# Sink attention and a routed attention mixture on one core: part of the loads and stores issued by ScalarE, other units by way of DRAM, and a new written-out order

## The chip, the cores and the metric

The kernel runs on one core of a Trainium2 chip. The core has a matrix engine (TensorE, in the profile PE, its weight loads PEld), a vector engine (VectorE, DVE), a scalar engine (ScalarE, ACT), a general engine (GpSimd, POOL) and an engine that here only issues transfers (SyncE, SP). Sixteen DMA engines move the data. An engine executes its instructions strictly in the order in which the program has them; across engines they wait for each other by semaphores. A transfer is started by an instruction that stands in the order of the engine that issues it.

The metric is the device time of one execution in microseconds (us), the median of some runs.

## The reference

Everything is float32, with inputs of 4 batches, 8 heads, 768 positions, head size 64. The first stage is a windowed attention in which each position sees the last 128 positions and the first 4 ("sinks"). Its output, heads side by side, is the input x (4 x 768 x 512) of the second stage: four "experts", each a causal attention with a head size of 64, weighted by a gate that keeps two experts for each position.

```python
keep = is_sink | in_window                      # 4 sinks, window 128
a = softmax(where(keep, q @ k.T / 8, -1e9))
x = (a @ v)                                     # heads side by side: 4 x 768 x 512
logits = x @ w_gate                             # two of four experts kept per position
for e in range(4):
    q, k, v = x @ wq[e], x @ wk[e], x @ wv[e]
    s = where(causal, -1e9, q @ k.T / 8)
    ye = softmax(s) @ v @ wo[e]
    out += weight_of(e) * ye                    # 0 where e is not among the two
```

## The kernel before

**Units.** The work is cut into units. A unit of the first stage, written (b, hp, 0), is one batch and one pair of heads (16 of them); a unit of the second stage, (b, ep, 1), is one batch and one pair of experts (8). In this document (b, ep) alone is a unit of the second stage. Sequences are cut into six blocks of 128 positions ("rows"). The two heads or experts of a pair use the two halves of the matrix engine.

**First stage** (`first`, `band_rows`, `edge_rows`, `both_rows`). q, k and v of a pair are loaded into natural-order tiles `qn`, `kn`, `vn` (three, two and three buffers). For batch 0 PE turns q and k (L1425, against the identity), for later batches the load brings 32 x 32 pieces and DVE turns them (L1323). Scores of the blocks come from L1348 and L1366, DVE takes the minimum and adds the mask (L1642, L1704), ACT makes the exponentials (L1647, L1708), POOL or ACT normalise, PE turns the probabilities (L1425), DVE or ACT move them to SBUF as `pt`, and PE multiplies them with v (L1392) and the sinks (L1396).

**Second stage** (`second`, `values`, `wide_rows`). x is kept as a high and a low part, and every product with weights is made of three (high with high, high with low, low with high): L1799 for queries and keys, L1826 for values and gate, L1873 for the output. Scores are L1353, DVE's mask and minimum L1570, exponentials L1578.

**Rows by way of DRAM.** A row block's probabilities must be turned before they meet v. For most blocks PE does it (`transposed`: L1425, then an evacuation to `pt`). For blocks 3, 4 and 5 of the units in `AWAY` (`by_way_of_dram`) the normalised block goes to `u` (three buffers), DVE turns it in 32 x 32 pieces (L1515, two instructions), one transfer writes it to DRAM as `there` (L1518), four read it back rearranged (L1522), and PE multiplies it with v (L1392, written `b<-u,v` in the trace). Five units of three blocks do this: (0,0), (0,1), (1,0), (1,1), (2,0).

**What sets the order.** Nothing is ordered by hand. Each piece of work is a `Step` with a priority, a cost in ns on each engine that could do it, the steps and buffers that it needs, and for a transfer the time `moves` that the DMA engines would take. `Plan.emit` plays a list scheduling: the engine that can start a step earliest takes one, PE by priority with a penalty for waiting and for changing the shape in which it is used. The result is only an order for each engine (and, for steps with two engines, the choice of one); the chip then runs these orders as fast as it can. Priorities get a correction from the table `NUDGE`, and `ONLY` pins steps to one engine; both are tables of numbers found by search. `ISSUE` multiplies the cost of SP's issues. Where the plan finds PE idle in the first 130 us of its own time, it puts in dummy matmuls on a tile of zeros (`fill`, L1037 the wide form, L1040 the narrow one); their results are never used.

**Transfers.** All are issued by SP, in one order: loads of q, k, v (L1763, and L1767 for 32 x 32 pieces, four instructions each), weights (L1151), the trips to DRAM and back (L1518, L1522), stores of the output (L1877). An issue that waits holds everything behind it on SP.

Of the kernel before, what the change touches and what calls it, by code (L numbers as in the profile page):

```python
# [1981 lines left out]
```

## Time and profile before

| | us |
|---|---|
| median of 3 runs (lowest, highest) | 380.84 (379.81, 382.02) |
| the profiled execution | 381.89 |
| its span, first to last instruction | 379.1 |
| PE busy | 360.7 (95%) |
| DVE busy | 292.6 (77%) |
| ACT busy | 271.0 (71%) |
| POOL busy | 196.3 (52%) |
| mean granted clock of PE | 0.989 |
| DMA, share of the sixteen engines | 52.5% on the kernel's queue |

The page divides the span into 40 slices of 9.5 us and gives for each the busy tenths of an engine, the clock granted to PE in tenths and the share of the DMA engines. A group's row gives its line, engine, tile names, shapes and count, then busy time and the mean ns of one, then the idle time of the engine just before and what ended it. A row of the waits reads: who waited for whom, us in total, times, the longest. A matmul in float32 counts as two in the trace. Matmuls overlap, so the mean of one is longer than the pace at which they follow each other; the pace is read from the pieces of the chain of waits.

### The profile page before, as it was taken

To read this page: it belongs to the slowest core of one execution; us is meant where nothing else is said; L and a number is where in the kernel's file an instruction comes from. 1 tells how busy PE (TensorE), PEld (TensorE's weight loads), DVE (VectorE), ACT (ScalarE), POOL (GpSimd) and SP (SyncE) were. 2 spreads that over 40 slices of the span, in tenths; PEclk is the share of its full clock that TensorE was granted. 3 is DMA by queue.
4 is the path that set the end of the run, shared out by engine and by line. 5 is a ranking of instruction groups with operands and counts; after the bars stand their busy time and mean duration, and the time that the engine had idled before them with its cause. 6 is when DMAs were issued, how large, how long until landed. Compare 5 with 4: busy or idle time off the path is not lost.

```text
span 379.1 us, 12937 instructions
## 1 busy us (share of the span) xinstructions
PE 360.7 (95%) x4642; PEld 310.3 (82%) x4642; DVE 292.6 (77%) x1272; ACT 271.0 (71%) x943; POOL 196.3 (52%) x474
## 2 busy tenths in 40 slices
PE   8988989999979998999998998999999999999996
PEld 7767878887768897978887887988888989988884
DVE  4898769779978978879987996649888936484951
ACT  2998959449967987448986975437999835068872
POOL 4398977949338733654655863142498510123410
PEclk9996999999999999999999999999999999999999
DMA  7998899904895686548965695026910000030012
GB/s 159 189 194 146 165 177 172 155 2 109 284 186 93 175 262 110 86 122 292 206 157 95 155 261 141 3 108 227 254 43 3 4 0 29 2 117 24 3 58 111
DMA packets 134832, 48.10 MB, mean 127 GB/s; under 512 B 121776, under 2 KB 129456, under 8 KB 134768
## 3 DMA queue, kind: packets, MB, share of 16 engines
q1 hardware_dynamic: 134768, 47.28, 52.5%
q8 instruction: 36, 0.59, 0.7%
q14 instruction: 28, 0.23, 0.2%
HBM read 30.88 MB, written 16.12 MB: 124 GB/s over the span
## 4 chain that ended last, share of the span: by engine, by line
PE 63%; DMA 10%; DVE 9%; ACT 6%; SPq 5%; POOL 4%; issue 2%; DVEq 0%; ACTq 0%
PE b L1392 15%; PE b L1873 9%; PE b L1799 9%; PE b L1353 7%; PE b L1826 7%; PE b L1425 7%; DMA u<-there 4%; DMA qn<-in_q_dram 3%; SPq L1767 3%; PE b L1348 3%; PE b L1366 3%; DMA there<-u 3%; SPq L1522 2%; ACT p L1708 2%; DVE u L1515 2%
## 5 line engine op out<-in xcount | busy, mean ns | idle before, releaser
L1578 ACT ACTIVATE p<-p,st 128x640 f32<-128x640 f32 (+5 forms) x96 | 63.6, 665 | 14.2 <-DVE st L1570 11.4
L1708 ACT ACTIVATE p<-p,st 128x132 f32<-128x132 f32 x128 | 50.8, 400 | 8.3 <-DVE st L1704 6.2
L1570 DVE CUSTOM_DVE_ANT_0 p<-b,cmask 128x384 f32<-128x384 f32 (+3 forms) x96 | 45.4, 501 | 2.4 <-PE b L1353 2.1
L1353 PE MATMUL b<-ks,qs 64*128 64x384 f32 (+3 forms) x384 | 44.3, 342 | 1.1 <-DVE st L1570 0.6
L1222 ACT ACTIVATE pt<-b 128x256 f32<-128x256 f32 (+3 forms) x99 | 38.8, 421 | 5.7 <-PE b L1425 5.3
L1425 PE MATMUL b<-ident,p 64*128 64x64 f32 x820 | 39.4, 227 | 0.2 <-DVE y L1210 0.2
L1392 PE MATMUL b<-pt,vn 128*64 128x128 f32 x448 | 39.0, 280 | 0.6 <-ACT pt L1222 0.5
L1224 DVE COPY pt<-b 128x256 f32<-128x256 f32 (+3 forms) x75 | 32.1, 450 | 8.3 <-PE b L1425 7.4
L1425 PEld LDWEIGHTS b<-ident,p 64*128 64x128 f32 x820 | 32.6, 138 | 6.8 <-issue 2.5
L1826 PE MATMUL b<-wvh,x 128*128 128x260 f32 x192 | 37.6, 286 | 0.2 <-DVE x L1210 0.2
L1408 POOL TENSOR_TENSOR st<-st 128x2 f32<-128x2 f32 (+1 forms) x52 | 10.2, 197 | 51.7 <-ACT p L1578 27.9
L1353 PEld LDWEIGHTS b<-ks,qs 64*128 64x128 f32 x384 | 30.9, 186 | 5.4 <-issue 1.6
L1726 POOL TENSOR_TENSOR p<-p,st 128x512 f32<-128x512 f32 x32 | 33.1, 1040 | 0.1
L1873 PE MATMUL b<-woh,y 128*128 128x512 f32 x96 | 32.8, 400 | 0.0
L1799 PE MATMUL b<-x,wkh 128*128 128x256 f32 (+1 forms) x128 | 32.7, 343 | 0.0
L1799 PE MATMUL b<-x,wqh 128*128 128x256 f32 (+1 forms) x128 | 32.6, 342 | 0.0
L1826 PEld LDWEIGHTS b<-wvh,x 128*128 128x128 f32 x192 | 30.6, 188 | 1.6 <-issue 0.6
L1704 DVE CUSTOM_DVE_ANT_0 p<-b,pair_mask 128x132 f32<-128x132 f32 x128 | 31.7, 283 | 0.0
L1647 ACT ACTIVATE p<-p,st 128x256 f32<-128x256 f32 (+1 forms) x64 | 28.6, 450 | 1.8 <-DVE st L1642 1.4
L1392 PEld LDWEIGHTS b<-pt,vn 128*64 128x64 f32 x448 | 25.4, 136 | 3.1 <-ACT pt L1222 0.8
L1366 PE MATMUL b<-kx,qn 64*64 64x196 f32 (+2 forms) x768 | 27.2, 286 | 0.0
L1826 PE MATMUL b<-wvl,x 128*128 128x260 f32 x96 | 27.1, 282 | 0.0
(133 smaller groups left out, 993.1 us busy)
## 6 DMA issues: line engine op xcount, KB each, us to landing
vn<-in_v_dram SPq DMA_DIRECT2D x32, 192.0 KB, 3.8
out_dram<-o SPq DMA_DIRECT2D x24, 256.0 KB, 2.0
qn<-in_q_dram SPq DMA_DIRECT2D x52, 96.0 KB, 3.2
kn<-in_k_dram SPq DMA_DIRECT2D x52, 96.0 KB, 2.5
there<-u SPq DMA_DIRECT2D x5, 768.0 KB, 4.1
u<-there SPq DMA_DIRECT2D x20, 192.0 KB, 5.1
there<-u SPq DMA_DIRECT2D x5, 640.0 KB, 2.9
u<-there SPq DMA_DIRECT2D x20, 160.0 KB, 3.8
```

Source lines behind the costliest of these rows:

```text
L1222: nc.scalar.activation(dst(), src(), AF.Copy)
L1353: nc.tensor.matmul(o, self.qs.t[hs, a, qs], keys(hs, b), start=n == 0, stop=n == 2)
L1366: nc.tensor.matmul(o, self.q_of()[hs, q0 + 64 * h:q0 + 64 * h + 64], ks, start=True, stop=True)
L1392: nc.tensor.matmul(o[e * 64:e * 64 + 64], lhs, rhs, start=e not in self.begun, stop=last and self.done == len(self.steps))
L1425: nc.tensor.transpose(t[g].t[:, n, :], x[gs], ident[gs, gs])
L1570: nc.vector.tensor_tensor_reduce(out=one(e)[:, cs], in0=s2[e].t[:, :(c1 - c0) * 128], in1=mask(c0, c1), scale=times, scalar=st.t[:, 3, es] ...
L1578: nc.scalar.activation(x, x, AF.Exp, bias=st.t[:, 0, es], scale=-1.0, accum_out=st.t[:, 1, es])
L1708: nc.scalar.activation(p.t[:, n, :], p.t[:, n, :], AF.Exp, bias=st.t[:, 0, n:n + 1], scale=-1.0, accum_out=st.t[:, 1, n:n + 1])
L1726: nc.gpsimd.tensor_mul(p.t[:, :, :128], p.t[:, :, :128], f()[:, :, None].to_broadcast([128, 4, 128]))
L1799: nc.tensor.matmul(t.t, w[a][:, c, es], X[b, c].t[:, x, cs], start=c == 0 and m == 0, stop=c == NCH - 1 and m == 2)
L1826: nc.tensor.matmul(t.t[:, :VW], X[b, c].t[:, a, qs], W["wv"][w][:, c, :], start=c == 0 and n == 0, stop=c == NCH - 1 and n == 2)
L1873: nc.tensor.matmul(t.t, Y[b, c].t[:, a, qs], W["wo"][w][:, c, :], start=c == 0 and n == 0, stop=c == EP - 1 and n == 2)
```

## The change

1. A new helper `transfer` makes a step that either SP or ACT may take, and issues the transfer on the engine that the plan (or `ONLY`) gave it. Loads of q, k, v and of the weights and stores of the output use it; the trips to DRAM and back stay on SP.
2. In the plan an issue on SP costs 1.4 times its figure (before 1.2), every transfer's DMA time is multiplied by 1.25, the end of every transfer comes 400 ns later, and transfers by ACT occupy the plan's DMA time too. Some figures of issues change (four loads of 32 x 32 pieces 2580 for 2124, two loads 1100 for 1062, reading back 2000 for 1900).
3. `AWAY` names (1,0), (1,1), (2,0), (2,1), (3,0): units (0,0) and (0,1) now have their blocks turned by PE, (2,1) and (3,0) go by way of DRAM.
4. `NUDGE` and `ONLY` are new throughout, and so are three weights of the order (`HURRY`, `STAY`, `BULK`). So the order of all engines is made anew.

The products that PE computes are the same in kind and number. In the order of the changed kernel 49 transfer instructions stand on ACT (15 of the 24 stores, 34 of loads); narrow dummy matmuls are 82 instead of 52, wide ones besides the opening ten 4 instead of 1. Of the two tables the diff shows two lines.

```diff
-ISSUE = 1.2
+ISSUE, MOVE_TIME, LANDING = 1.4, 1.25, 400
...
 ONLY = {
-    "000 fn_DVEACT 0": DVE, "000 fn_DVEACT 2": ACT, "000 fn_DVEACT 5": ACT, "000 fn_DVEACT 6": ACT, "000 fn_DVEACT 7": DVE,
+    " load_SPACT 0": SP, " load_SPACT 4": SP, " load_SPACT 5": SP, "000 load_SPACT 0": ACT, "000 load_SPACT 1": SP,
...
-HURRY = 79.02
-STAY = 46.95
-BULK = 0.96
+HURRY = 86.86
+STAY = 50.53
+BULK = -58.78
...
-        self.prio, self.cost, self.fn, self.new, self.moves, self.mode = prio, cost, fn, new, moves, mode
+        self.prio, self.cost, self.fn, self.new, self.moves, self.mode = prio, cost, fn, new, moves * MOVE_TIME, mode
...
-            if e == SP:
+            if s.moves:
                 moved = max(moved, t + 1000) + s.moves
-                free[SP] = max(s.end, moved - 2500)
-                s.end = max(moved + 1000, s.end + 1800)
+                if e == SP:
+                    free[SP] = max(s.end, moved - 2500)
+                s.end = max(moved + 1000, s.end + 1800) + LANDING
...
+    def transfer(prio, many, each, fn, *rest, queues=(SP, ACT), **more):
+
+        def go():
+            fn((nc.scalar if s.eng == ACT else nc.sync).dma_start)
+        go.__qualname__ = fn.__qualname__
+        s = plan.step(prio, {q: many * each for q in queues}, go, *rest, **more)
+        return s
...
-            ld = plan.step(prio, {SP: 530 * many}, load, new=[st], fifo=tag, moves=2400 * whole / 1024)
+            ld = transfer(prio, many, 530, load, new=[st], fifo=tag, moves=2400 * whole / 1024)
...
-        got = plan.step(prio - WIDE_N - 10, {SP: 1900}, back, [s], (), [there, u], moves=2 * MOVE * n)
+        got = plan.step(prio - WIDE_N - 10, {SP: 2000}, back, [s], (), [there, u], moves=2 * MOVE * n)
...
-                loaded[-1].append((a, z, [plan.step(
-                    load_prio + (0.1 if n else 0.2 if which == 2 else 0), {SP: 1062 if which == 2 or by_pe else 2124}, load, (), [] if n else [t],
+                loaded[-1].append((a, z, [transfer(
+                    load_prio + (0.1 if n else 0.2 if which == 2 else 0), *((2, 550) if which == 2 or by_pe else (4, 645)), load, (), [] if n else [t],
...
-        plan.step(prio, {SP: 410}, lambda: nc.sync.dma_start(out[b, qs, :], o.t), [moved], (), [o], moves=650)
+        transfer(prio, 1, 410, lambda start: start(out[b, qs, :], o.t), [moved], (), [o], moves=650)
...
-    AWAY, MOVE = {u: (3, 4, 5) for u in ((0, 0), (0, 1), (1, 0), (1, 1), (2, 0))}, 250
+    AWAY, MOVE = {u: (3, 4, 5) for u in ((1, 0), (1, 1), (2, 0), (2, 1), (3, 0))}, 250
```

More of the change, by code (lines that the diff above doesn't have):

```diff
@@ new lines @@
+    "000 load_SPACT 2": SP, "000 load_SPACT 3": ACT, "000 load_SPACT 4": SP, "000 fn_DVEACT 1": ACT, "000 fn_DVEACT 3": ACT,
+    "000 fn_DVEACT 4": DVE, "000 fn_DVEACT 5": ACT, "000 fn_DVEACT 6": DVE, "000 fn_DVEACT 7": DVE,
+    "000 total_DVEPOOL 0": POOL, "000 norm_POOLACT 0": POOL, "000 norm_POOLACT 1": POOL, "000 fn_DVEACT 8": DVE,
+    "000 total_DVEPOOL 1": DVE, "000 fn_DVEACT 10": ACT, "000 fn_DVEACT 11": DVE, "000 fn_DVEACT 13": DVE,
+    "000 total_DVEPOOL 2": POOL, "000 fn_DVEACT 15": DVE, "000 fn_DVEACT 16": DVE, "000 fn_DVEACT 17": ACT,
@@ new lines @@
+    "030 fn_DVEACT 4": ACT, "030 fn_DVEACT 5": ACT, "030 fn_DVEACT 7": DVE, "030 norm_POOLACT 0": ACT,
+    "030 norm_POOLACT 1": ACT, "030 fn_DVEACT 8": ACT, "030 fn_DVEACT 10": ACT, "030 fn_DVEACT 12": DVE,
+    "030 fn_DVEACT 13": DVE, "030 total_DVEPOOL 2": DVE, "030 fn_DVEACT 14": DVE, "030 fn_DVEACT 15": DVE,
+    "030 fn_DVEACT 16": DVE, "030 fn_DVEACT 17": ACT, "110 load_SPACT 0": SP, "110 load_SPACT 1": SP,
+    "110 load_SPACT 2": SP, "110 total_DVEPOOL 0": DVE, "110 norm_POOLACT 0": POOL, "110 norm_POOLACT 1": ACT,
@@ new lines @@
+    "110 fn_DVEACT 0": DVE, "110 fn_DVEACT 1": ACT, "110 total_DVEPOOL 1": DVE, "110 fn_DVEACT 4": DVE,
+    "110 total_DVEPOOL 2": DVE, "110 fn_DVEACT 8": DVE, "110 fn_DVEACT 9": ACT, "100 load_SPACT 0": SP,
+    "100 load_SPACT 1": SP, "100 load_SPACT 2": ACT, "100 total_DVEPOOL 0": POOL, "100 norm_POOLACT 0": ACT,
+    "100 norm_POOLACT 1": POOL, "100 fn_DVEACT 1": ACT, "100 total_DVEPOOL 1": DVE, "100 fn_DVEACT 2": ACT,
+    "100 fn_DVEACT 3": ACT, "100 fn_DVEACT 6": ACT, "100 fn_DVEACT 8": ACT, "100 fn_DVEACT 9": ACT, "001 fn_DVEACT 1": ACT,
@@ new lines @@
+    "001 fn_DVEACT 2": ACT, "001 fn_DVEACT 3": ACT, "001 fn_DVEACT 4": ACT, "001 fn_DVEACT 5": DVE,
+    "001 norm_POOLACT 0": ACT, "001 norm_POOLACT 1": POOL, "001 fn_DVEACT 6": ACT, "001 norm_POOLACT 3": ACT,
+    "001 fn_DVEACT 9": DVE, "001 total_DVEPOOL 2": DVE, "001 norm_POOLACT 4": POOL, "001 norm_POOLACT 5": POOL,
+    "001 fn_DVEACT 11": ACT, "001 total_DVEPOOL 3": POOL, "001 norm_POOLACT 6": POOL, "001 norm_POOLACT 7": POOL,
+    "001 fn_DVEACT 12": DVE, "001 total_DVEPOOL 4": POOL, "001 norm_POOLACT 8": ACT, "001 norm_POOLACT 9": POOL,
@@ new lines @@
+    "001 fn_DVEACT 14": ACT, "001 fn_DVEACT 15": ACT, "001 total_DVEPOOL 5": DVE, "001 fn_DVEACT 18": DVE,
+    "001 fn_DVEACT 19": ACT, "001 fn_DVEACT 20": DVE, "001 fn_DVEACT 21": ACT, "120 load_SPACT 0": SP,
+    "120 load_SPACT 1": SP, "120 load_SPACT 2": ACT, "120 norm_POOLACT 0": POOL, "120 fn_DVEACT 0": DVE,
+    "120 total_DVEPOOL 1": DVE, "120 total_DVEPOOL 2": DVE, "120 fn_DVEACT 6": DVE, "120 fn_DVEACT 7": DVE,
+    "120 fn_DVEACT 8": ACT, "120 fn_DVEACT 9": ACT, "130 load_SPACT 0": SP, "130 load_SPACT 1": ACT,
@@ new lines @@
+    "130 load_SPACT 2": ACT, "130 total_DVEPOOL 0": POOL, "130 norm_POOLACT 0": ACT, "130 fn_DVEACT 0": DVE,
+    "130 fn_DVEACT 2": ACT, "130 fn_DVEACT 3": ACT, "130 fn_DVEACT 4": ACT, "130 fn_DVEACT 6": ACT, "130 fn_DVEACT 7": ACT,
+    "130 fn_DVEACT 9": DVE, "011 norm_POOLACT 1": ACT, "011 fn_DVEACT 0": DVE, "011 fn_DVEACT 1": ACT,
+    "011 fn_DVEACT 2": ACT, "011 total_DVEPOOL 2": POOL, "011 fn_DVEACT 4": ACT, "011 total_DVEPOOL 3": POOL,
+    "011 norm_POOLACT 7": POOL, "011 fn_DVEACT 6": ACT, "011 norm_POOLACT 9": ACT, "011 fn_DVEACT 11": DVE,
@@ new lines @@
+    "011 norm_POOLACT 10": POOL, "011 norm_POOLACT 11": ACT, "011 fn_DVEACT 12": ACT, "011 fn_DVEACT 13": DVE,
+    "011 fn_DVEACT 14": ACT, "011 fn_DVEACT 15": ACT, "011 fn_DVEACT 16": ACT, "011 store_SPACT 1": SP,
+    "011 fn_DVEACT 18": DVE, "011 fn_DVEACT 19": ACT, "011 store_SPACT 3": ACT, "011 fn_DVEACT 20": ACT,
+    "011 fn_DVEACT 21": ACT, "011 store_SPACT 5": ACT, "210 load_SPACT 1": SP, "210 load_SPACT 2": SP,
+    "210 total_DVEPOOL 0": DVE, "210 norm_POOLACT 0": POOL, "210 norm_POOLACT 1": POOL, "210 fn_DVEACT 0": DVE,
@@ new lines @@
+    "101 norm_POOLACT 5": POOL, "101 fn_DVEACT 6": DVE, "101 norm_POOLACT 6": ACT, "101 norm_POOLACT 7": POOL,
+    "101 total_DVEPOOL 4": POOL, "101 norm_POOLACT 9": POOL, "101 norm_POOLACT 10": ACT, "101 norm_POOLACT 11": ACT,
+    "101 fn_DVEACT 11": ACT, "220 load_SPACT 1": SP, "220 total_DVEPOOL 0": POOL, "220 norm_POOLACT 1": POOL,
+    "220 fn_DVEACT 0": ACT, "220 total_DVEPOOL 1": DVE, "220 fn_DVEACT 2": DVE, "220 fn_DVEACT 4": DVE,
+    "220 fn_DVEACT 5": ACT, "220 total_DVEPOOL 2": POOL, "220 fn_DVEACT 6": ACT, "220 fn_DVEACT 7": ACT,
@@ new lines @@
+    "230 load_SPACT 0": SP, "230 load_SPACT 1": ACT, "230 load_SPACT 2": SP, "230 fn_DVEACT 1": ACT,
+    "230 total_DVEPOOL 1": DVE, "230 fn_DVEACT 4": ACT, "230 fn_DVEACT 5": DVE, "230 fn_DVEACT 6": ACT,
+    "111 total_DVEPOOL 0": POOL, "111 norm_POOLACT 2": POOL, "111 norm_POOLACT 3": POOL, "111 total_DVEPOOL 2": DVE,
+    "111 norm_POOLACT 4": POOL, "111 fn_DVEACT 0": DVE, "111 fn_DVEACT 1": ACT, "111 total_DVEPOOL 3": POOL,
+    "111 norm_POOLACT 7": POOL, "111 norm_POOLACT 9": ACT, "111 fn_DVEACT 2": DVE, "111 fn_DVEACT 3": ACT,
@@ new lines @@
+    "111 total_DVEPOOL 5": POOL, "111 norm_POOLACT 10": ACT, "111 norm_POOLACT 11": POOL, "111 fn_DVEACT 5": ACT,
+    "111 fn_DVEACT 6": ACT, "111 store_SPACT 0": SP, "111 fn_DVEACT 7": DVE, "111 store_SPACT 1": ACT,
+    "111 fn_DVEACT 8": ACT, "111 fn_DVEACT 9": ACT, "111 store_SPACT 3": ACT, "111 fn_DVEACT 10": ACT,
+    "111 store_SPACT 4": ACT, "300 load_SPACT 0": SP, "300 load_SPACT 1": SP, "300 load_SPACT 2": ACT,
+    "300 norm_POOLACT 1": ACT, "300 fn_DVEACT 2": DVE, "300 fn_DVEACT 3": ACT, "300 fn_DVEACT 5": DVE,
@@ new lines @@
+    "201 fn_DVEACT 9": ACT, "201 total_DVEPOOL 5": DVE, "201 norm_POOLACT 11": POOL, "201 fn_DVEACT 10": DVE,
+    "201 fn_DVEACT 11": DVE, "310 load_SPACT 0": SP, "310 norm_POOLACT 0": ACT, "310 norm_POOLACT 1": POOL,
+    "310 fn_DVEACT 0": ACT, "310 fn_DVEACT 1": ACT, "310 fn_DVEACT 3": DVE, "310 fn_DVEACT 5": ACT,
+    "310 total_DVEPOOL 2": DVE, "310 fn_DVEACT 6": ACT, "310 fn_DVEACT 7": ACT, "310 fn_DVEACT 8": ACT,
+    "310 fn_DVEACT 9": ACT, "320 load_SPACT 0": SP, "320 load_SPACT 1": ACT, "320 load_SPACT 2": SP,
@@ new lines @@
+    "320 total_DVEPOOL 0": POOL, "320 fn_DVEACT 0": DVE, "320 fn_DVEACT 1": DVE, "320 total_DVEPOOL 1": DVE,
+    "320 fn_DVEACT 4": DVE, "320 fn_DVEACT 5": ACT, "320 fn_DVEACT 6": ACT, "320 fn_DVEACT 8": DVE, "320 fn_DVEACT 9": ACT,
+    "330 load_SPACT 0": SP, "330 load_SPACT 1": SP, "330 norm_POOLACT 0": POOL, "330 fn_DVEACT 0": ACT,
+    "330 total_DVEPOOL 1": POOL, "330 fn_DVEACT 3": ACT, "330 fn_DVEACT 5": ACT, "330 total_DVEPOOL 2": DVE,
+    "330 fn_DVEACT 6": ACT, "330 fn_DVEACT 8": ACT, "211 total_DVEPOOL 0": DVE, "211 norm_POOLACT 0": ACT,
@@ new lines @@
+    "211 fn_DVEACT 10": ACT, "211 store_SPACT 4": SP, "211 fn_DVEACT 11": ACT, "301 fn_DVEACT 1": DVE,
+    "301 fn_DVEACT 2": DVE, "301 fn_DVEACT 4": ACT, "301 fn_DVEACT 5": ACT, "301 norm_POOLACT 1": ACT,
+    "301 norm_POOLACT 2": POOL, "301 norm_POOLACT 3": POOL, "301 norm_POOLACT 4": ACT, "301 norm_POOLACT 5": POOL,
+    "301 total_DVEPOOL 3": POOL, "301 norm_POOLACT 7": POOL, "301 total_DVEPOOL 4": POOL, "301 norm_POOLACT 8": POOL,
+    "301 norm_POOLACT 9": POOL, "301 fn_DVEACT 8": DVE, "301 total_DVEPOOL 5": POOL, "301 norm_POOLACT 10": ACT,
@@ L1758, in first, with load @@
             for n, (a, z) in enumerate([(0, 3), (3, NB)] if whole and which < 2 else [(0, NB)]):
-                def load(t=t, src=src, which=which, a=a, z=z):
+                def load(start, t=t, src=src, which=which, a=a, z=z):
                     for e in range(2):
@@ L1762, in load @@
                         if which == 2 or by_pe:
[L1763 removed]
+                            start(t.t[:, a:z, e, :], x.rearrange("(t p) d -> p t d", p=128)[:, a:z, :])
                             continue
```

142 lines of the change are left out of this document (45 added, 97 removed), and 1333 rows, old and new, of the table NUDGE.

## The prediction

> **What bounds the kernel now.** I read the page's shares first, then the clock and DMA lines of its slices, then PE's waits, then the stretches in which PE is not full.
>
> ```profile
> PE 360.7 (95%) x4642; PEld 310.3 (82%) x4642; DVE 292.6 (77%) x1272; ACT 271.0 (71%) x943; POOL 196.3 (52%) x474
> PEclk9996999999999999999999999999999999999999
> DMA  7998899904895686548965695026910000030012
> PE 63%; DMA 10%; DVE 9%; ACT 6%; SPq 5%; POOL 4%; issue 2%; DVEq 0%; ACTq 0%
> ```
>
> PE is busy for 360.7 of 379.1 us, so all its gaps together are 18.4 us. The change keeps every product that PE computes, so it can win gaps, half-speed time and dummy matmuls, and nothing else. The chain of waits gives DMA and SP's queue 15% together, far more than PE's gaps: most of those transfers lie beside PE work that was there anyway. DMA is crowded to about slice 27 and nearly free afterwards.
>
> The first 100 us and the rest differ (columns: PE, PEld, DVE, ACT, POOL busy, clock, DMA share, GB/s):
>
> ```profile
> 0.00:70.00 70.00, 63.57 (x965) 53.47 (x967) 55.65 (x297) 55.16 (x228) 51.46 (x119) 0.95 0.89 171
> 70.00:100.00 30.00, 29.58 (x340) 24.62 (x337) 26.32 (x101) 19.00 (x62) 22.37 (x49) 1.00 0.42 109
> 28.00:30.00 2.00, 1.30 (x15) 0.88 (x15) 2.00 (x18) 2.00 (x10) 1.92 (x4) 0.91 0.57 97
> 30.00:32.00 2.00, 1.69 (x14) 1.34 (x13) 1.94 (x6) 2.00 (x11) 1.92 (x7) 0.50 1.06 170
> 32.00:34.00 2.00, 2.00 (x34) 1.54 (x34) 1.15 (x8) 1.73 (x8) 1.40 (x2) 0.50 0.81 167
> 34.00:36.00 2.00, 2.00 (x36) 1.67 (x30) 1.46 (x4) 1.28 (x7) 1.92 (x5) 0.50 1.02 186
> 36.00:38.00 2.00, 2.00 (x26) 1.57 (x23) 2.00 (x16) 1.49 (x7) 1.44 (x3) 0.88 0.55 100
> ```
>
> Up to 70 us PE lacks 6.43 us, to 100 us another 0.42: 6.85 us of gaps, most of them where DVE, ACT and DMA are all near full. And there is one stretch at half clock: 0.18 x 2 + 6 + 0.24 x 2 = 6.84 us, which did 3.4 us of full-speed work. So the early stage lost 3.4 us to the clock.
>
> Later, PE's gaps are almost only these:
>
> ```profile
> PE b L1392 <- DMA u<-there: 6.8, 5, 1.9
> 113.09 1.09 PE L1392 MATMUL b<-u,v 128*64 128x128 f32 x16 [1.93 <-DMA u<-there]
> 144.01 1.53 PE L1392 MATMUL b<-u,v 128*64 128x128 f32 x24 [0.53 <-DMA u<-there]
> 147.49 1.09 PE L1392 MATMUL b<-u,v 128*64 128x128 f32 x16 [1.29 <-DMA u<-there]
> 200.88 1.09 PE L1392 MATMUL b<-u,v 128*64 128x128 f32 x16 [1.40 <-DMA u<-there]
> 233.14 1.53 PE L1392 MATMUL b<-u,v 128*64 128x128 f32 x24 [1.66 <-DMA u<-there]
> ```
>
> Five of the fifteen row blocks that go by way of DRAM come back too late, 1.36 us each on average. The remaining 18.4 - 6.85 - 6.8 = 4.7 us are mostly the tail after PE's last matmul.
>
> **Term 1, rows by way of DRAM.** The five units move from (0,0), (0,1), (1,0), (1,1), (2,0) to (1,0), (1,1), (2,0), (2,1), (3,0). Five units of 15 blocks stay five, so PE's transposes only move: no term. What counts is PE's cover, the work that stands in PE's order between the last score step that the block's turn can need and its product with v. I priced the order's rows with these merged pieces of the chain (the kinds by line: projections, values, output, scores, transposes, products):
>
> ```profile
> 338.13 8.64 PE b L1799 x48
> 238.67 7.02 PE b L1826 x57
> 369.67 5.83 PE b L1873 x24
> 351.88 1.64 PE b L1353 x18
> 366.42 0.89 PE b L1425 x24
> 367.31 2.36 PE b L1392 x40
> 261.78 1.51 PE b L1366 x40
> 256.99 0.71 PE b L1348 x8
> 271.47 0.59 PE b L1396 x4
> ```
>
> That is 0.18, 0.123, 0.243, 0.091, 0.037, 0.059, 0.038, 0.089 and 0.147 us apiece (fp32 products count twice in the trace). Before, the five late blocks have covers of 18.7, 14.4, 16.5, 17.0 and 16.0 us; with a cover of 17.5 us or less four of six waited. In the change three of fifteen are that short (17.5, 17.1, 15.8), the others reach from 17.8 to 44.7, and six blocks lie where DMA was nearly idle before. Two of the three late at 1.36 us is 2.7 us of waiting, so I take -4.0 us; the ends are 0 (the waits only move) and -6.8. PE's order at the fourth unit by DRAM, (1,1) before and (2,1) now (u is a block read back from DRAM, pt one turned by PE), before:
>
> ```order
> L1392 MATMUL b_126<-pt_104,v_0_83 64x128 x6
> L1392 MATMUL b_132<-u_94,v_0_83 64x128 x10
> L1392 MATMUL b_132<-u_95,v_0_83 64x128 x12
> L1392 MATMUL b_128<-pt_103,v_0_83 64x128 x2
> L1392 MATMUL b_128<-pt_105,v_0_83 64x128 x4
> L1392 MATMUL b_126<-u_96,v_0_83 64x128 x8
> ```
>
> and now:
>
> ```order
> L1424 MATMUL b_125<-pt_105,v_0_83 64x128 x6
> L1424 MATMUL b_131<-pt_103,v_0_83 64x128 x2
> L1424 MATMUL b_131<-pt_104,v_0_83 64x128 x4
> L1424 MATMUL b_128<-u_94,v_0_83 64x128 x10
> L1424 MATMUL b_128<-u_96,v_0_83 64x128 x12
> L1424 MATMUL b_125<-u_95,v_0_83 64x128 x8
> ```
>
> All three blocks read back now come behind the turned ones; covers go from 23.2, 16.0, 18.1 to 20.6, 18.0, 19.4 us.
>
> **Term 2, the clock, and term 3, dummy matmuls.** PE's order in the first attention stage, after the scores of the third head pair (kx_81, qn_67), before:
>
> ```order
> L1366 MATMUL b_128<-kx_81,qn_67 64x68
> L1366 MATMUL b_125<-kx_81,qn_67 64x68
> L1366 MATMUL b_128<-kx_81,qn_67 64x2x64
> L1366 MATMUL b_125<-kx_81,qn_67 64x2x64
> L1425 MATMUL b_126<-ident,qn_65 128x64
> L1425 MATMUL b_130<-ident,qn_65 128x64
> ```
>
> and now:
>
> ```order
> L1398 MATMUL b_125<-kx_81,qn_67 64x68
> L1398 MATMUL b_130<-kx_81,qn_67 64x68
> L1398 MATMUL b_125<-kx_81,qn_67 64x2x64
> L1398 MATMUL b_130<-kx_81,qn_67 64x2x64
> L1064 MATMUL b_126<-nought 64x128 x28
> L1457 MATMUL b_126<-ident,qn_65 128x64
> L1457 MATMUL b_127<-ident,qn_65 128x64
> ```
>
> 28 dummies now fill the place after which PE halved its clock. The row before the drop:
>
> ```profile
> 26.00:28.00 2.00, 1.09 (x31) 0.78 (x21) 2.00 (x15) 2.00 (x9) 2.00 (x1) 1.00 1.03 220
> 6.36 0.81 PE b L1040 x12
> ```
>
> PE was busy for 1.09 and 1.30 of 2 us and then fell to 0.50. I count half of the 3.4 us as won, -1.7 (ends 0 and -3.4), because ACT and DVE are nearly full there and take up part of it. The Trainium skill, "TensorE: Matmul & The Clock Gate", section "What's actually happening", says that the clock halves after at least one idle window of about 3.4 us. Here it fell after four microseconds that were 60% busy, so the trace is stricter than the rule; by the rule alone term 2 would be 0 and the sum 1.7 us higher.
>
> In all there are 30 more narrow dummies (82 for 52) and 3 more wide ones at the very start. The narrow ones are 60 in the trace's count, 0.81/12 = 0.0675 us each: 4.05 us. The wide ones lie in PE's wait for the first load. As much as 6.85 us of gaps could hold the narrow ones, none need do so: ends 0 and +4.05; I take +1.5, since the 28 take 3.8 us where the three windows from 26 to 32 us had gaps of 0.91 + 0.70 + 0.31 = 1.9 us.
>
> **Term 4, ScalarE issues.** 49 of the DMA instructions leave SP: 15 stores and 34 for loads. What they cost on ACT no row shows; the nearest are SP's (count, then ns min/median/max):
>
> ```profile
> L1877 SPq DMA_DIRECT2D out_dram<-o x24: 332/333/840, 165.4 to 376.2; - x24
> L1763 SPq DMA_DIRECT2D vn<-in_v_dram x32: 368/486/2543, 5.0 to 274.3; - x32
> L1767 SPq DMA_DIRECT2D kn<-in_k_dram x48: 311/524/2997, 29.0 to 206.5; - x48
> ```
>
> 15 x 0.333 + 34 x 0.5 = 22 us, behind which ACT's own work queues. The new order takes some normalising calls from ACT to POOL in return:
>
> ```profile
> L1231 ACT ACTIVATE p<-p,st 128x128 f32<-128x128 f32 (+5 forms) x32 | 18.5, 593 | 5.8 <-POOL st L1417 5.8
> L1657 ACT ACTIVATE p<-p,st 128x128 f32<-128x128 f32 (+1 forms) x30 | 11.6, 446 | 4.6 <-DVE st L1413 4.6
> ```
>
> Twelve fewer of the first kind (with the u forms) and six of the second are about 10 us, five more output evacuations at 0.6 us give 3 back. ACT ends near 271 + 22 - 7 = 286 us, 75%: no bound on average. Locally it can be late; I take +1.0, with ends -1.0 (less normalising in a full stretch) and +8.0 (the second rival). ACT's order around the first projections, before and then now (L1708/L1740 are exponentials, v_0_83 evacuations that PE needs):
>
> ```order
> L1222 ACTIVATE pt_104<-b_127 128x4x64
> L1157 ACTIVATE wkh<-o_114 128x260
> L1708 ACTIVATE p_87,st_123<-p_87,st_123 128x132 x3
> L1222 ACTIVATE v_0_83<-b_128 128x256
> L1708 ACTIVATE p_93,st_119<-p_93,st_119 128x132 x2
> ```
>
> ```order
> L1740 ACTIVATE p_87,st_122<-p_87,st_122 128x132
> L1799 DMA qn_66<-in_q_dram 32x24x32 x4
> L1740 ACTIVATE p_93,st_124<-p_93,st_124 128x132
> L1254 ACTIVATE v_0_83<-b_125 128x256
> L1689 ACTIVATE p_92<-p_92,st_123 128x128 x2
> L1799 DMA kn_69<-in_k_dram 32x24x32 x4
> L1254 ACTIVATE v_0_83<-b_131 128x256
> L1189 ACTIVATE woh<-o_114 128x260
> L1795 DMA vn_70<-in_v_dram 128x6x64 x2
> ```
>
> Ten issues stand here between evacuations, and four more some twenty rows earlier.
>
> **Term 5, loads earlier.** SP no longer holds a load behind a store that waits.
>
> ```profile
> PE b L1348 <- DVE qn L1323: 1.3, 1, 1.3
> ```
>
> That is the one PE wait behind a late load after the start; I take -0.7, ends 0 and -2.0 (with part of the start). "DMA: Bandwidth & Descriptors" in the Trainium skill, "Issuing engines are not separate DMA queues", says that issuing from several engines saves only the sequencer's time, which is usually small. By it the term is 0 and the sum 0.7 us higher; no run so far shows two queues. The constants 1.4, 1.25, 400 and the changed issue costs act only through the order, so they have no term of their own; the new order's unknown waits I put at 0, between -2 and +3.
>
> Sum: -4.0 - 1.7 + 1.5 + 1.0 - 0.7 = -3.9 us. The span becomes 375.2 us; the profiled execution took 381.89, 2.79 more than its span, so 378.0; the median of the runs is 1.05 below that execution: 377.0 us.
>
> **Rivals.** (a) Everything lands: waits to 1 us, clock held, dummies in gaps: -5.8 - 3.4 - 0.7 = -9.9, about 371 us. For it: PE has work without a gap from 240 us on. Against: the early stage is crowded on ACT and DVE too. (b) Nothing net: late blocks stay late at other places (three covers of 17.5 us or less) and the dummies cost their 4.05 us: -2.7 - 1.7 + 4.05 + 1.0 - 0.7 = 0, near 381 us. (c) Slower: ACT's queue stands still. Fourteen issues lie around the first projections, where DMA is at 0.95; held like SP's slow ones, say 1.1 us each, they take 15.4 us.
>
> ```profile
> 60.00:70.00 10.00, 10.00 (x133) 8.62 (x135) 8.79 (x45) 9.29 (x43) 7.67 (x20) 1.00 0.95 164
> 70.00:80.00 10.00, 9.82 (x83) 9.02 (x79) 6.36 (x22) 2.64 (x11) 9.53 (x24) 1.00 0.48 87
> ```
>
> ACT has 7.4 us free from 70 to 80 us; the other 8.0 delay PE: -4.9 + 8.0 = +3.1, 384 us. It decides from (7.4 + 4.9)/14 = 0.88 us an issue. Against it: SP's medians of about 0.5.
>
> **Chances.** About 0.5% (1.9 us) is what this kernel's measurement tells from none. Forecast 0.41, (a) 0.13, (b) 0.24, (c) 0.22. Faster: 0.54; same: (b), 0.24; slower 0.22. The likeliest's own range is 374 to 379. The range reaches most of (a) and (c): 371 to 385.
>
> **What would show it.** Right: PE's wait for u at about 2.7 us; the clock near 1.00 from 28 to 38 us; dummies 164 in the trace; ACT near 286 us of work and issues with medians as SP's. Wrong: PE waiting for ACT's evacuations at 65 to 85 us, issues on ACT above 0.88 us, a half-clock stretch still there or elsewhere, or more than 7 us lost by 100 us.

## The result and the profile after

The changed kernel takes 368.44 us (median of 4 runs, 368.14 to 369.11); the kernel before took 380.32 us beside it. The ratio is 0.9683, with an interval from 0.9647 to 0.972: 11.9 us faster, three times the 3.9 us that were forecast, and below the range. The profiled execution has a span of 366.2 us, 12.9 us less than before.

The page of the changed kernel: PE's busy time (the first row), the clock and DMA shares of 40 slices, the shares of the chain of waits, and the two hardware queues (packets, MB, share of 16 engines; q10 is ScalarE's).

```profile
PE 357.6 (98%) x4708; PEld 311.1 (85%) x4708; DVE 288.4 (79%) x1271; ACT 262.3 (72%) x928; POOL 206.3 (56%) x490
PEclk9999999999999999999999999999999999999999
DMA  9983988961281218322897898018920463049512
PE 87%; DVE 6%; ACT 3%; DMA 2%; issue 1%; SPq 0%; ACTq 0%; DVEq 0%
q1 hardware_dynamic: 108000, 38.75, 45.9%
q10 hardware_dynamic: 26768, 8.52, 9.7%
```

PE's gaps shrink from 18.4 to 366.2 - 357.6 = 8.6 us, and the clock is full in every slice. The DMA engines are no emptier in all (45.9 + 9.7% for 52.5%), but their crowded slices have moved: the 11th to the 19th slice, from about 95 to 175 us, were at 0.4 to 0.9 before and are now at 0.1 to 0.3 but for two, and the traffic reappears behind them. DMA and SP's queue, 15% of the chain before, are 2%.

The longest of PE's six waits in the changed kernel (the others are of 1.1 us, at the very start, and of 0.6 us and less):

```profile
PE b L1398 <- POOL kx L1328: 1.5, 1, 1.5
```

The wait for u, 6.8 us before, is not among them at all. By stages, the kernel before from 100 us on and the changed one (columns as in the prediction: PE, PEld, DVE, ACT, POOL busy, clock, DMA share, GB/s):

```profile
100.00:160.00 60.00, 55.62 (x754) 49.13 (x753) 50.37 (x225) 46.85 (x174) 30.48 (x77) 1.00 0.73 166
160.00:250.00 90.00, 86.54 (x1058) 75.20 (x1057) 72.76 (x302) 63.49 (x214) 44.49 (x108) 1.00 0.61 154
250.00:380.00 130.00, 125.40 (x1538) 107.93 (x1536) 87.46 (x349) 86.50 (x269) 47.49 (x125) 0.99 0.22 70
```

```profile
0.00:70.00 70.00, 65.12 (x1052) 55.24 (x1053) 56.21 (x305) 52.28 (x216) 57.37 (x128) 1.00 0.86 159
70.00:100.00 30.00, 30.00 (x415) 26.10 (x417) 27.34 (x123) 22.99 (x79) 19.18 (x46) 1.00 0.47 86
100.00:160.00 60.00, 60.00 (x778) 53.56 (x771) 45.59 (x199) 41.11 (x152) 33.60 (x82) 1.00 0.43 84
160.00:250.00 90.00, 90.00 (x1121) 78.04 (x1119) 77.84 (x317) 66.65 (x226) 51.58 (x122) 1.00 0.59 148
250.00:380.00 130.00, 112.51 (x1362) 98.19 (x1359) 81.42 (x331) 79.28 (x257) 44.61 (x114) 0.99 0.42 123
```

From 70 to 250 us PE has no gap. Up to 70 us its gaps fall by 1.55 us, up to 100 us by another 0.42; behind 100 us they fall from 279.1 - 267.56 = 11.5 to 266.2 - 262.51 = 3.7 us. That is 9.8 us of gaps. The other 3.1 us are less busy time, although the dummies' busy time grew by 3.6 us (11.8 for 8.2): 3.4 of it answers to the half-clock stretch, and some 3.3 us are the same products running closer together. No run has a cause for these by itself; run 12 below, the kernel before without its trips to DRAM, has 358.8 us of busy time at a mean clock of 0.988 (before 360.7 at 0.989), so that 1.9 us of them go together with the trips.

### The profile page after: what moved, and what is told of

It reads as the page before. It is cut to its first block, busy times and chain, and to the rows that moved or that the text cites. A ratio compares the mean times of both kernels' runs of the same rounds, so it can differ in the third digit from the quotient of the medians.

```text
span 366.2 us, 13040 instructions
## 1 busy us (share of the span) xinstructions
PE 357.6 (98%) x4708; PEld 311.1 (85%) x4708; DVE 288.4 (79%) x1271; ACT 262.3 (72%) x928; POOL 206.3 (56%) x490
## 3 DMA queue, kind: packets, MB, share of 16 engines
q1 hardware_dynamic: 108000, 38.75, 45.9%
## 4 chain that ended last, share of the span: by engine, by line
PE 87%; DVE 6%; ACT 3%; DMA 2%; issue 1%; SPq 0%; ACTq 0%; DVEq 0%
PE b L1424 21%; PE b L1831 19%; PE b L1385 10%; PE b L1858 10%; PE b L1905 9%; PE b L1457 8%; PE b L1398 5%; PE b L1380 3%; PE b L1428 1%; DVE b L1728 1%; ACT p L1740 1%; DVE p L1736 1%; DVE p L1674 1%; DMA kn<-in_k_dram 1%; DMA qn<-in_q_dram 1%
## 5 line engine op out<-in xcount | busy, mean ns | idle before, releaser
L1610 ACT ACTIVATE p<-p,st 128x256 f32<-128x256 f32 (+5 forms) x96 | 63.5, 665 | 10.1 <-DVE st L1602 9.7
L1457 PE MATMUL b<-ident,p 64*128 64x64 f32 x820 | 38.5, 227 | 0.3 <-POOL p L1758 0.3
L1256 DVE COPY pt<-b 128x256 f32<-128x256 f32 (+3 forms) x74 | 33.3, 464 | 4.8 <-PE b L1457 2.7
L1679 ACT ACTIVATE p<-p,st 128x128 f32<-128x128 f32 (+1 forms) x64 | 28.9, 454 | 5.5 <-DVE st L1674 5.3
L1831 PE MATMUL b<-x,wqh 128*128 128x512 f32 (+1 forms) x128 | 32.8, 341 | 0.0
L1514 POOL TENSOR_SCALAR_AFFINE_SELECT pt<-pt 128x512 f32<-128x512 f32 x32 | 20.3, 635 | 13.4 <-ACT pt L1254 8.9
L1398 PE MATMUL b<-kx,qn 64*64 64x128 f32 (+2 forms) x768 | 26.1, 277 | 1.5 <-POOL kx L1328 1.5
```

The lines of the kernel that those rows point to most:

```text
L1398: nc.tensor.matmul(o, self.q_of()[hs, q0 + 64 * h:q0 + 64 * h + 64], ks, start=True, stop=True)
L1457: nc.tensor.transpose(t[g].t[:, n, :], x[gs], ident[gs, gs])
L1610: nc.scalar.activation(x, x, AF.Exp, bias=st.t[:, 0, es], scale=-1.0, accum_out=st.t[:, 1, es])
L1831: nc.tensor.matmul(t.t, w[a][:, c, es], X[b, c].t[:, x, cs], start=c == 0 and m == 0, stop=c == NCH - 1 and m == 2)
```

## The experiments

The text "expected" stands as it was recorded ahead of each run. A block that is not sent by way of DRAM, or is read back to another place, reaches its product in the wrong order; that part of the computation is left out in runs 4, 5, 6, 9, 10, 11 and 12. An edit that adds or takes lines moves the numbers of those behind it: L1323 of the kernel before is L1324 in run 6 and L1355 in the changed kernel.

### Runs 1 to 4: one part at a time

Run 1, the changed kernel with every transfer issued by SP:

```diff
-            fn((nc.scalar if s.eng == ACT else nc.sync).dma_start)
+            fn(nc.sync.dma_start)
```

> The changed kernel; the 49 transfer instructions that its plan gives to ScalarE are issued by SyncE instead, at the places that the plan gives them; the orders of all other engines stay. Theory (the order of PE and the places of the DRAM rows bring the gain, the second issuing engine little): 368 to 371 us, PE's gaps grow by less than 2 us. Rival (two issuing engines bring loads earlier and free SyncE from waiting stores, and that is most of the gain): 374 us or more, with PE waiting for loads or for rows read back. A gain below 368 would mean that ScalarE's issues cost more than they bring.

Measured: 368.08 us, ratio to before 0.9672 (0.9643 to 0.9702), the changed kernel's own. PE waits for almost the same things. The second issuing engine brings nothing that the measurement tells.

Run 2, the changed kernel without its dummies (the opening ten stay):

```diff
-FILL_COST, FILL_KEEP, FILL_END = 220.0, 0.0, 130000.0
+FILL_COST, FILL_KEEP, FILL_END = 220.0, 0.0, 0.0
```

> The changed kernel without the dummy matmuls that the plan inserts (82 narrow, 4 wide); the opening ten stay, and so do all orders. Theory (dummies hold the clock and lie in gaps): the granted clock falls to half somewhere before 70 us, and the time is 370 to 373 us. Rival (the dummies only cost their 4 to 6 us of PE): 363 to 367 us with a clock near 1.00.

Measured: 374.48 us, ratio 0.9821 (0.9779 to 0.9863): about half of the gain is gone (5.2 us by the ratios, 6.0 by the medians), and the time lies above the 370 to 373 us that were expected. The window shows how:

```profile
0.00:70.00 70.00, 58.00 (x842) 47.59 (x843) 53.26 (x292) 49.55 (x204) 52.43 (x121) 0.85 0.77 145
```

PE has 7.1 us more of gaps up to 70 us, where the dummies were, and a mean clock of 0.85.

Run 3, the kernel before with the 28 narrow dummies ahead of the transposes at 28 us:

```diff
+            if e == PE and s.part[-1] == "030 tr_PE 0":
+                ...                       # one row of 14 pairs of narrow products on zeros
```

> The kernel before with 28 narrow dummies (14 pairs) ahead of the transposes of the fourth head pair, the place at which the change has them; nothing else moves. Theory (half the early gain is the clock): the clock stays near 1.00 from 28 to 38 us and the time falls by 2 to 3.4 us, to 377 to 378.5. Rival (DVE, ACT and DMA bound that stage, the clock costs nothing): 380 to 381, clock held or not.

Measured: 378.77 us, ratio 0.9949 (0.991 to 0.9988), 1.9 us less by the ratio (0.5 to 3.4 by its interval). The row holds the clock where it fell before; in this execution it fell elsewhere, beside waits for u (5.4 us of PE's time in all):

```profile
28.00:38.00 10.00, 8.42 (x150) 6.96 (x148) 6.97 (x38) 7.08 (x32) 6.89 (x15) 1.00 0.84 148
130.00:150.00 20.00, 18.00 (x256) 16.36 (x256) 13.95 (x61) 15.36 (x58) 5.17 (x21) 0.91 0.79 197
```

Run 4, the kernel before with neither the write to DRAM nor the reading back:

```diff
-        s = plan.step(..., lambda: nc.sync.dma_start(there.t, whole()), turns, ...)
+        s = plan.step(..., lambda: None, turns, ...)
...
-                nc.sync.dma_start(u.t[32 * b:32 * b + 32]..., there.t...[b])
+            pass
```

> The kernel before, leaving out the writes to DRAM and the reads back of its fifteen row blocks (their products with v use the block as VectorE left it); all orders stay, SyncE only lacks these transfers. Theory (the trips' lateness is worth what PE's wait shows): 6.8 us and a little more, 372 to 374.5 us. Rival (other waits follow behind, so taking the trips away gives less than half of it): 377 us or more. Below 371 would mean that the trips also slow other transfers on the path.

Measured: 371.33 us, ratio 0.9763 (0.9717 to 0.9809). The trips cost the kernel before 9.0 us, more than all its waits for u (6.8). One window of the profile shows it, where PE was full for 7.45 us of ten before:

```profile
110.00:120.00 10.00, 10.00 (x172) 9.04 (x172) 9.92 (x42) 8.32 (x32) 7.38 (x20) 1.00 0.51 82
```

### Run 5: both together

The kernel before with the edits of runs 3 and 4.

> The kernel before with both single edits of the earlier runs together: the rows that went by way of DRAM are neither written nor read back (their product takes the block as VectorE left it, so that part of the output is not the attention's), and 28 narrow products on zeros stand ahead of the transposes at 28 us. Alone the first took 9.0 us and the second 1.6 us. Theory (the two causes are all of the change, and they add): 380.3 - 9.0 - 1.6 = 369.7 us, and up to 3 us less if the fast clock, which in the run with the products alone fell again at 130 to 150 us beside a wait for u, stays up once that wait is gone. Rival (something else in the new order, as the issues by ScalarE or the earlier loads, holds a part): over 371 us.

Measured: 370.34 us, ratio 0.9712 (0.9675 to 0.9748). The change's interval is 0.9647 to 0.972, so the two are not told apart. The two edits, made in the old order without any replanning, give 11.4 us (11.0 by the ratio); the new order gives 11.9. The rival, over 371 us, falls by little: on the 380.33 us that it was worked out from, the interval reaches 370.7 us. Where the kernel before lacked 4.4 us, PE is full, as in the changed kernel:

```profile
100.00:160.00 60.00, 60.00 (x790) 53.30 (x789) 54.14 (x241) 47.40 (x174) 32.77 (x84) 1.00 0.37 66
```

### Runs 6, 9, 10 and 12: what of a trip costs

Run 6, the kernel before with the whole trip, but read back to a place that nobody reads, so that PE waits for nothing:

```diff
+    aside = [dram.tile([128, 1536], F32, name=f"aside_{x}") for x in range(3)]
...
-                nc.sync.dma_start(u.t[32 * b:32 * b + 32].rearrange("r a e x -> r a (e x)"),
+                nc.sync.dma_start(aside[u.slot][32 * b:32 * b + 32, :u.t.shape[1] * u.t.shape[2] * u.t.shape[3]].rearrange("r (a x) -> r a x", a=4),
                                   there.t.rearrange("(a r) (b x) -> b r a x", a=4, b=4)[b])
```

> The kernel before with the whole trip kept on the queue and in the DMA engines, but read back into a place in DRAM that nobody reads; the product takes the block as VectorE left it, so that it waits for no transfer and that part of the output is not the attention's. Theory (the trip costs by its waits and by crowding other transfers): the 6.8 us of shown wait go and the crowding stays, about 373.5 us. Rival (only the wait counts, and what follows from it): 371.3 us as without the trip. Rival (the trip costs by its traffic): over 376 us.

Measured: 381.67 us, ratio 1.0006 (0.9966 to 1.0047). This was my theory's worst miss: with the 6.8 us of wait taken away and the traffic left, nothing is won; the rival of the traffic holds. Two things take the place of the wait. PE's gaps shrink by only 3.1 us (from 18.4 to 377.9 - 362.6 = 15.3), since other waits come, and the clock halves a second time. In the kernel before, and then in this run, VectorE's wait for the loads of q and SP's own for the write (with the median time of two kinds of write to land):

```profile
DVE qn L1323 <- DMA qn<-in_q_dram: 10.3, 7, 2.5
SPq L1522 <- DMA there<-u: 12.7, 8, 2.8
there<-u SPq DMA_DIRECT2D x5, 768.0 KB, 4.1
there<-u SPq DMA_DIRECT2D x5, 640.0 KB, 2.9
```

```profile
DVE qn L1324 <- DMA qn<-in_q_dram: 11.1, 7, 2.5
SPq L1523 <- DMA there<-u: 9.7, 6, 2.7
110.00:120.00 10.00, 7.80 (x103) 6.28 (x100) 8.17 (x33) 5.28 (x20) 7.14 (x18) 1.00 0.85 149
120.00:130.00 10.00, 10.00 (x129) 8.81 (x125) 8.88 (x36) 8.73 (x30) 6.88 (x13) 0.83 0.33 104
```

SP's row is that of its own order: before it may read back, it stands in its order until the write has landed, and the next unit's loads queue behind it. The third row shows PE still with 2.2 us of gaps in the window where run 4 had none, and the fourth the clock at 0.83 right behind them, where the kernel before had 1.00. Over all executions the mean clock of run 6 is 0.9835 in the median and that of the kernel before beside it 0.990: an estimated 380 x 0.0065 = 2.5 us of run 6 are clock. SP's order in the kernel before, at the first trips (start, length, transfer, count), and the same load in run 4:

```profile
100.71 2.27 SPq L1522 DMA_DIRECT2D u<-there  x4
103.08 4.49 SPq L1767 DMA_DIRECT2D qn<-in_q_dram  x4
107.61 3.00 SPq L1522 DMA_DIRECT2D u<-there  x4
```

```profile
99.40 2.04 SPq L1765 DMA_DIRECT2D qn<-in_q_dram  x4
```

The load of q starts 3.7 us later beside the trips, and its four issues take 4.49 us for 2.04.

Run 9, as run 6, but the block read back comes from the input q, so that SP need not stand for the write; bytes and counts stay:

```diff
-                                  there.t.rearrange("(a r) (b x) -> b r a x", a=4, b=4)[b])
+                                  q[0, b][:128 * n].rearrange("(a r y) d -> r a (y d)", a=4, y=n))
```

> As the second run of the last group (the kernel before, rows written to DRAM and a block of the same size read back into a place that nobody reads, PE not waiting for it, so that part of the output is not the attention's), but the block that is read back is taken from the input q instead of the rows just written: SyncE need no longer stand until the write has landed, and the bytes and the count of transfers stay. That run took 381.7 us as the kernel before did, and VectorE's waits for loads of qn were 11.1 us in it against 4.4 without the trips. Theory (the trips cost because SyncE stands still before each read-back and the loads of qn queue behind it): qn waits near 5 us, 374 to 377 us. Rival (the transfers' own time in the DMA engines and on SyncE): qn waits stay at 9 us or more, 380 to 382 us.

Run 10, as run 6, but each write and each reading back carries the first 1 KB of every row alone:

```diff
-        ... nc.sync.dma_start(there.t, whole()) ...
+        ... nc.sync.dma_start(there.t[:, :256], whole()[:, :256]) ...
```

> As the same run (unwaited trips in the kernel before, part of the output not the attention's), but each write and each read-back carries only the first 1 KB of every row instead of 5 or 6 KB: the instructions, their order and SyncE's stand for the landing stay, the bytes fall to a fifth or a sixth. Theory (SyncE's standing and its issues make the loads late): qn waits stay near 9 us and the time at 379 us or more. Rival (the bytes in the DMA engines do): qn waits near 4.4 us, 372 to 374 us. Between: both, in proportion.

Run 12, the kernel of run 4 once more, on the chip of runs 9 and 10:

> The kernel before without the trips once more, on the same chip as the two thinner ones, so that the three stand against one another: 371.3 us as the first time, VectorE's waits for qn 4.4 us.

The waits of VectorE for q in runs 9, 10 and 12:

```profile
DVE qn L1324 <- DMA qn<-in_q_dram: 8.2, 6, 2.5
```

```profile
DVE qn L1324 <- DMA qn<-in_q_dram: 4.8, 5, 1.9
SPq L1523 <- DMA there<-u: 5.8, 3, 3.5
there<-u SPq DMA_DIRECT2D x15, 128.0 KB, 2.2
```

```profile
DVE qn L1323 <- DMA qn<-in_q_dram: 3.0, 2, 2.0
```

| | PE waits for u | bytes of the trips | SP stands for the write, us | VectorE waits for q, us | time, us | ratio (interval) |
|---|---|---|---|---|---|---|
| before | yes | all | 12.7 | 10.3 | 381.63 | |
| run 6 | no | all | 9.7 | 11.1 | 381.67 | 1.0006 (0.9966 to 1.0047) |
| run 9 | no | all | 0 | 8.2 | 376.45 | 0.9868 (0.9814 to 0.9921) |
| run 10 | no | a fifth | 5.8 | 4.8 | 372.06 | 0.9751 (0.9727 to 0.9776) |
| run 12 | no | none | 0 | 3.0 | 371.52 | 0.9744 (0.9723 to 0.9765) |

(Run 6 ran beside another series of the kernel before, 381.76 us.) Run 10's rival holds, and run 9's theory half: the 75 instructions of the trips cost nothing that the noise shows by themselves (run 10 against 12), the bytes carry nearly the whole price, and about half of it (5.2 of 10.1 us) goes when SP need not stand for the landing. Some 2.9 of these 5.2 us are the clock that run 6 loses and run 9 does not, by an estimate from their mean clocks (0.9835 and 0.991 in the median). The two prices overlap, since thin writes land sooner (2.2 us for 2.9 to 4.1).

Time and VectorE's wait for q fall together in the five kernels of the table. The row of a single profile scatters, though: run 4, the same kernel as run 12, has 4.4 us of this wait at 371.33 us. That the late loads of q carry the price is read from this row; no run made those loads early and left everything else. Where more than the trips was changed, the two part: runs 14 and 15 below have 5.1 and 4.6 us of this wait and are slower than the kernel before.

### Run 8: one row of dummies

The changed kernel without its longest row of dummies (28 of 82):

```diff
-                    order.append((free[PE], len(order), f))
+                    if int(spare / FILL_COST) < 14:
+                        order.append((free[PE], len(order), f))
```

> The changed kernel without its one long row of narrow products on zeros (28 of them, 3.28 us at 28.6 us); the other rows stay. Theory (that row keeps the fast clock through the stretch that ran at half clock before): half clock for some 3.5 us between 28 and 36 us, 370 us. Rival (all the rows together hold it, none by itself): 368.4 us. Rival (the row is most of what the run without any rows lost): 372 us or more.

Measured: 371.27 us, ratio 0.9746 (0.9699 to 0.9794): the row is worth 2.4 us by the ratios and 2.8 by the medians, half of what run 2 lost. The windows around it, with the row (the changed kernel) and then without, and pieces of PE's timeline (start, length, count, idle time ahead and what ended it):

```profile
30.00:32.00 2.00, 2.00 (x40) 1.83 (x38) 1.61 (x16) 2.00 (x8) 1.77 (x2) 1.00 0.04 8
32.00:34.00 2.00, 0.79 (x24) 0.65 (x22) 1.47 (x6) 2.00 (x11) 1.90 (x3) 1.00 0.00 0
34.31 0.90 PE L1398 MATMUL b<-kx,qn 64*64 64x196 f32 x24 [1.52 <-POOL kx L1328]
```

```profile
30.00:32.00 2.00, 1.17 (x12) 0.79 (x12) 2.00 (x18) 2.00 (x8) 1.79 (x2) 1.00 0.00 0
32.00:34.00 2.00, 0.06 (x1) 0.00 (x0) 1.00 (x5) 2.00 (x11) 1.90 (x3) 0.62 0.00 0
34.00:36.00 2.00, 1.72 (x26) 1.38 (x28) 0.82 (x6) 1.29 (x6) 1.86 (x7) 0.50 0.67 143
30.80 1.26 PE L1458 MATMUL b<-ident,kn 64*128 64x64 f32 x12 [1.60 <-DVE st L1737]
34.28 1.58 PE L1399 MATMUL b<-kx,qn 64*64 64x196 f32 x24 [2.23 <-POOL kx L1329]
```

The dummies take time in which PE had nothing else to do: the scores behind them start at 34.31 us with the row and at 34.28 us without, since they wait for kx from GpSimd either way. All that they change is the clock at which the scores run: the same 24 products take 0.90 and 1.58 us.

### Runs 7, 13, 14: issues by ScalarE in the old order

The kernel before with the 28 steps by name that ScalarE issues in the change, each where SP issued it (52 instructions, since one name is that of a larger load of weights here); runs 13 and 14 do the 15 stores and the 13 load steps, 37 instructions, alone:

```diff
-                    nc.sync.dma_start(to, src)
+                    (nc.scalar if plan.now in BY_ACT else nc.sync).dma_start(to, src)
```

> The kernel before with the same 28 loads and stores issued by ScalarE as in the changed kernel, each at the place in the plan where SyncE issued it; nothing else moves. My step (49 issues on ScalarE cost 1.0 us in all): 381.3 us. Theory after the first run (the engine that issues is of no account): 380.3 us. Rival (SyncE relieved, the trip's transfers issue sooner and the waits for u shrink): 377 to 379 us. Rival (a load waits for its buffer in ScalarE's order and the work behind it stands): over 383 us.

> The kernel before with only its 15 stores (of the 28 steps of the run that cost 7 us) issued by ScalarE. Each takes 0.34 us of ScalarE's order, 5 us in all, at 166 us and later. Theory (the loads do the harm, since they stand early, where ScalarE is full, and wait for buffers in its order): 381 to 382 us, as before. Rival (the stores do it, by standing ahead of evacuations and exponentials in the second stage): 385 us or more.

> The kernel before with only its 13 load steps (30 instructions of ScalarE, most before 110 us) issued by ScalarE. Theory (the loads do the harm): 386 to 389 us. Rival (stores): 381 to 383 us. Between: both, in proportion.

Measured: 388.8 us for all, ratio 1.0202 (1.0154 to 1.0249); 381.05 us for the stores, 1.0028 (0.9984 to 1.0071); 386.83 us for the loads, 1.0142 (1.0071 to 1.0213). The loads do the harm, 5 to 6 us of it. Run 14 up to 70 us:

```profile
0.00:70.00 70.00, 61.59 (x923) 51.60 (x924) 53.99 (x278) 52.38 (x214) 48.14 (x110) 0.93 0.87 164
```

PE has done 2.0 us less by then than in the kernel before, at 0.93 of its clock for 0.95. The rest of the loss was not traced to a place. The same kind of transfers, placed by a plan that knows of them, cost nothing (run 1).

### Run 11: the trips in the new order

The changed kernel with the edit of run 4.

> The changed kernel without the write to DRAM and the read-back (the product takes the block as VectorE left it, so that part of the output is not the attention's). Theory (in the new order the trips lie where few loads follow, and cost nothing any more): 367.5 to 368.5 us, the same. Rival (they still crowd the loads or PE's transposes): 366 us or less.

Measured: 368.44 us, ratio 0.9665 (0.9645 to 0.9686). In the new order the trips, the same 15 blocks and as many bytes, cost nothing.

### Run 15: the trips issued by GpSimd

The kernel before with the five transfers of each trip on GpSimd, PE waiting as before:

```diff
-        ... nc.sync.dma_start(there.t, whole()) ...
+        ... nc.gpsimd.dma_start(there.t, whole()) ...
...
-                nc.sync.dma_start(u.t[32 * b:32 * b + 32]...
+                nc.gpsimd.dma_start(u.t[32 * b:32 * b + 32]...
```

> The kernel before with the five transfers of each trip issued by GpSimd instead of SyncE, at the same place of the plan; PE waits for the block as before and the output is the attention's. SyncE no longer stands for the landing, and the loads of qn do not queue behind the trips; the bytes stay. Theory (standing is half of the trips' price, as the run with another source showed): qn waits of VectorE 8 us or less, 375 to 379 us, if GpSimd, 52% busy, can bear to stand in SyncE's place. Rival (GpSimd's normalising queues behind the landing instead): 381 us or more.

Measured: 397.69 us, ratio 1.0432 (1.0362 to 1.0503). The rival holds:

```profile
DVE qn L1323 <- DMA qn<-in_q_dram: 4.6, 4, 2.4
PE b L1392 <- DMA u<-there: 9.2, 6, 2.4
PE b L1425 <- POOL p L1233: 3.2, 2, 2.8
L1522 POOL DMA_DIRECT2D u<-there x60: 550/550/625, 97.4 to 284.8; - x60
```

With SP free VectorE waits less for q (4.6 for 10.3 us), but 75 issues of 0.55 us (reading back) and 0.62 us (writing) in the median now stand in GpSimd's order, its normalising comes late, and PE waits more. This fits that the trips on SP hold back the loads of q. It does not show it, since everything else of this kernel comes later too, nor what it would be worth alone.

## Why the prediction was wrong, step by step

**What bounds the kernel.** The frame held in the main: gaps gave 9.8 us and the clock 3.4 of the span's 12.9, and the dummies took 3.6 us more. Two things were wrong in it. I wrote "and nothing else", and 3.3 us are products running closer together; and I let the gaps behind 100 us be worth the one wait named in them.

**Term 1, rows by way of DRAM: the step that failed.** Forecast -4.0 with -6.8 as its far end; the trips cost 9.0 us (run 4) and 10.1 (run 12) in the old order, and in the new one nothing (run 11). The end of -6.8 was wrong in kind: I took PE's wait for u as the whole price of the trips. Run 6 shows that this wait is not even the price: without it the time stays, because of other waits and the clock. The price goes with the bytes: trips with a fifth of them cost nothing that is measured (run 10, 372.06 us against 371.52 without trips). A sign of what I should have priced stood in VectorE's waits, 10.3 us for q in 7 pieces, and in SP's order. The covers decided less than I made of them: three short ones were to leave 2.7 us of wait, and there is none, though reading back takes no less time. The issues of the readings back, and their time to landing, in the kernel before and then in the changed one:

```profile
L1522 SPq DMA_DIRECT2D u<-there x60: 303/432/1662, 98.4 to 271.0; - x60
DMA to landing us min/median/max: 2.6/4.1/6.4
```

```profile
L1554 SPq DMA_DIRECT2D u<-there x60: 302/430/1785, 177.6 to 337.6; - x60
DMA to landing us min/median/max: 2.7/4.6/7.0
```

What changed is the place. Reading back begins at 177.6 us instead of 98.4, so that 12 load instructions of q come behind the first of it, where 28 did; SP stands 5.1 us for the writes instead of 12.7. That this place, and not another part of the new order, makes the trips free is argued from these rows: no run put the old units into the new order or the new ones into the old.

**Term 2 and term 3, clock and dummies.** Forecast -1.7 and +1.5, together -0.2. Measured together -1.9 in the old order (run 3, between -3.4 and -0.5) and -2.4 to -2.8 in the new one for the same row (run 8). The clock is held as "right" foresaw (1.00 from 28 to 38 us, 164 dummies in the trace). The size of term 3 failed: I let dummies that do not fit into the gaps of the old order push work back, but in the new order the work behind the row of 28 waits for kx until 34.3 us anyway, so that this row costs 0, the lower end. And all rows of dummies together are worth 5 to 6 us (run 2); I priced only those added.

**Term 4, issues by ScalarE.** The durations came out as SP's, as I had estimated:

```profile
L1909 ACTq DMA_DIRECT2D out_dram<-o x15: 338/339/375, 146.9 to 363.2; - x15
L1799 ACTq DMA_DIRECT2D kn<-in_k_dram x12: 318/537/538, 70.8 to 200.8; - x12
```

ScalarE's 262.3 us busy and some 22 us of issues are near the 286 I gave. The effect on the time is 0 for the forecast +1.0 (run 1), within its ends. Rival (c), which term 4 calls the second, did not come. In an order not made for it much the same edit does cost 7 us (run 7), but that this is near the rival's 8.0 is chance: the rival had ACT's queue hold up PE at 60 to 80 us, and there PE is as busy in run 14 (9.88 and 9.81 of 10 us) as in the kernel before (10.00 and 9.82). Of the 2.0 us that it lacks by 70 us, 1.9 were lost before 60 us.

**Term 5, loads earlier.** Forecast -0.7 for a second issuing engine; it gives nothing (run 1). The Trainium skill, "DMA: Bandwidth & Descriptors", section "Issuing engines are not separate DMA queues", has it that only the sequencer's time for the issue is saved, usually little, and run 1 agrees. The loads of q did come earlier. VectorE waited 10.3 us for them before, and waits 0.2 us in run 1 (all issued by SP). Its wait in the changed kernel and in run 11 (no trips):

```profile
DVE qn L1355 <- DMA qn<-in_q_dram: 4.0, 1, 4.0
```

```profile
DVE qn L1355 <- DMA qn<-in_q_dram: 3.7, 1, 3.7
```

So the second engine is not what made them early, and the 4.0 us that are left come neither from the trips nor do they cost time: run 1 is without them and takes as long. That is a warning about this row as well: not every us of it is a us of the kernel. The gain was booked nowhere: I read PE's wait behind a late load (1.3 us) and not VectorE's wait for the load itself.

**The rivals.** (a), everything lands, about 371 us, is nearest; it had the right parts, and term 1 too small for the same reason. I gave it 0.13 because the early stage is crowded on ACT and DVE; it is, but the dummies there needed neither. (b) and (c) did not come.

The sum with measured terms, the trips' price being that of the old order: trips -9.0 to -10.1, clock and dummies -1.9 to -2.8, issues and loads 0, together -10.9 to -12.9; measured -11.9. The new constants of the plan by themselves stay open: the two tables of numbers were made together with their constants and units, and no order with one of these undone was tried.
